# Transposes between groups of experts: one run of three or four tiles on TensorE in place of runs of two, with the third and fourth tile in banks of the first layers' ring

## The chip, the cores and the metric

One NeuronCore of one Trainium2 chip runs the whole program in one launch. The metric is the device time of one execution in microseconds, as the median of several; lower is better. TensorE is called PE here, VectorE DVE, ScalarE ACT, GpSimd POOL and SyncE SP, as in the profile.

## The reference

The program computes sliding-window attention with sink tokens, and feeds its output into a mixture of experts in two levels. Cut to the second part, which the change is in:

```python
x = attention(q, k, v).transpose(0, 2, 1, 3).reshape(3072, 512)
g_idx = argmax(x @ w_group)                   # one of 4 groups, weight g_w = its softmax
e_idx = argmax(xg @ w_expert[g])              # one of 4 experts in it, weight e_w = its softmax
h  = maximum(x[tok] @ w1[g, e], 0.0)          # 512 -> 1024, for the tokens of one expert
ye = h @ w2[g, e]                             # 1024 -> 512
out[tok] = (g_w * e_w)[:, None] * ye
```

All tensors are fp32. There are 16 experts; each token goes through exactly one.

## The kernel before, in words

**Stages.** Attention over 24 tiles of 128 tokens fills the first 150 us or so. Each tile's rows are written to a DRAM scratch, and routing on DVE builds lists of tokens. The experts are then worked off in order of how many tokens they got: r0 is the largest, r15 the smallest, and `CAPT` (L48) gives the slots of each. `PARTS` (L76 to L82) is the list of groups in that order: r0, r1, r8, r2 (in two parts), r9, r3 with r14, r10, r4 with r15, r5, r11, r6 with r12, r7 with r13. The change touches the places between the groups from r9 on.

**Precision.** A weight or an activation is split into a high part (`whi`, rounded to fp32r) and the rest (`wlo`); products hi·hi, hi·lo and lo·hi are summed in PSUM. The split of a 128x1024 block of weights is one cast on ACT (`whi<-rw`) and one subtraction on DVE (`wlo<-rw,whi`); activations are split likewise into a tile `un`. Small experts (r14, r15, at most 64 slots: "plain") and the remainder rows of r3, r4, r8 to r11 (`FEW`) use the raw fp32 weights instead.

**One group.** First layers write to `ph`, a ring of four PSUM banks (L1312). Then come the second layers, tile by tile of 128 tokens, into `po`, a ring of two (L1375): `layer2` (L1133) issues for each of 8 blocks f three matmuls of 512 columns. Where a group's first expert has remainder rows, `layer2` stops after f = 1, and `rest_of` (L1199) and `few_tokens` (L1113) do those rows in 16 matmuls in a bank that `spare()` (L207) takes from the `ph` ring; in the trace they are the `ph<-rw,hq` matmuls. A second ring of two banks, `ps_t` (L1374), holds transposes, and `bank(ps_t)` (L194) takes one.

**The pieces between.** Two kinds of work need PE transposes between the first layer of one group and the first layer of the next. A move, `xpose` (L928), takes 128 gathered token rows of the next group (`xg`, fetched by indirect DMA one group earlier), transposes them in four blocks into one PSUM bank, and has ACT and DVE split them into `un` (for a plain expert ACT copies them to `xr`), and DVE copy the gate `cg`. Rows of a small tile can share the transposes of another (`TWIN`, L90). `hidden_t` (L1084) transposes one half, four blocks, of the hidden layer `hs` of a plain or narrow expert of the present group; ACT (and DVE, if not plain) take them out. `hs` itself is made at the end of that expert's first layer (`layer1_plain`, L1034): ACT copies one strip of PSUM and DVE adds the other strips, one for 64 slots and three for 32 slots, for each half of 512 columns.

**Their order.** The list `todo` of such pieces is cut into runs of two (L1414). A run is issued whole by `pop_todo` (L1099), after every so many blocks f of the second layers, or by `pop_front` (L1105), ahead of the remainder rows at f = 1. Where there are remainder rows, the moves come first in the list, and otherwise the hidden pieces. All engines work in program order (`Pinned`, L126), so a piece that PE must wait for holds up everything behind it on PE. When the weight casts are issued is set by a planner's clock (`spend`, L916), to which each move adds some DVE time.

The pieces at each place, with the rows of each transpose:

- behind r9: r3 (128, 128) and r14 with a twin (96); then runs of 2 and 1
- behind r3 with r14: r10 (128, 32), hidden of r14 (two halves, 64 rows); runs of 2 and 2
- behind r10: r4 (128, 128), r15 with a twin (64); runs of 2 and 1
- behind r4 with r15: r5 (128, 96), hidden of r15 (two halves, 32 rows); runs of 2 and 2
- behind r11: r6 (128, 64), r12 (128); runs of 2 and 1
- behind r6 with r12: hidden of r12 (two halves, 128 rows), r13 (128), r7 (128, 64); runs of 2, 2 and 1

All other places have two pieces or fewer, or are behind r0.

Of the kernel before, what the change touches and what calls it, by code (L numbers as in the profile page):

```python
# [89 lines left out]
TWIN = {(3, 2): (14, 0, 64), (4, 2): (15, 0, 32), (9, 1): (2, 3, 96)}  # L90
# [53 lines left out]
def drain(g):  # L144
    for _ in g:
        pass


def moe_attention(tc, kqT, vN, vS, nsw, wgx, wgd, w1, w2, out):
    nc = Pinned(tc)  # L150
    v = nc.vector
    with ExitStack() as top, ExitStack() as att:
# [9 lines left out]
        ps_t = None  # L162
# [31 lines left out]
        def bank(pt):  # L194
            return pt.tile([P, 4, P], F32, name="tp")
# [11 lines left out]
        def spare():  # L207
            return tail[0].tile([P, 512], F32, name="ph")
# [466 lines left out]
        def dve(us):  # L675
            state["dve"] = max(state["dve"], state["clk"]) + us
# [218 lines left out]
        def routing(k, kinds=(None, "pe", "rd")):  # L895
            while k > 0:
                if not rb or not have.issuperset(rb[0][0]):
                    return False
                kind = rb[0][2] if isinstance(rb[0][2], str) else None
                if kind not in kinds or (kind == "pe" and state["clk"] < state["at"]):  # L900
                    return False
                rb[0][2] = r = next(rb[0][1], "end")
                k -= r if isinstance(r, int) else 1
                if tail:
                    dve(0.6 if kind == "rd" else 0.25)
                state["at"] = max(state["clk"] + state["gap"], state["dve"] + 0.4)
                if rb[0][2] == "end":
                    rb.pop(0)
            return True

        def wait_for(key):
            while key not in ready:
                state["clk"] += 0.3
                routing(1)
# [13 lines left out]
        def xpose(q, j, early=False):  # L928
            r, w = (q["r"], q["j0"] + j), min(P, q["T"] - j * P)
            if r in TWIN:  # L930
                return
            src = xg[r]
            both = [(q, j, 0, w)] + [tenants[a] + b[2:] + (32,) for a, b in TWIN.items() if b[0:2] == r]
            rows = sum(x[3] for x in both)
            tx = spare().rearrange("p (a b) -> p a b", a=NDC) if early else bank(ps_t)
            for c in range(NDC):
                nc.tensor.transpose(tx[:, c, 0:rows], src[0:rows, c * P:(c + 1) * P], ident[0:rows, 0:rows])
            for q, j, p, w in both:
                T, o, t = q["T"], q["o"], tx[:, :, p:p + w]
                dve(0.3 + 0.5 * w / P)  # L940
                cg[q["r"], q["j0"] + j] = gate = gp.tile([P, 1], F32, name="cg", bufs=10)
                if q["plain"]:
                    q["x"] = a = yp.tile([P, NDC, 64], F32, name="xr", bufs=1)[:, :, 0:w]
                    nc.scalar.copy(a, t)
                elif q["r"] in WHOLE:
                    q["x"] = a = yp.tile([P, NDC, q["n"]], F32, name="xw", bufs=1)
                    nc.scalar.copy(a, t[:, :, 0:q["n"]])
                else:
                    a = xx[:, :, o + j * P:o + j * P + w]
                    nc.scalar.copy(a, t)  # L950
                    v.tensor_tensor(xx[:, :, o + T + j * P:o + T + j * P + w], t, a.bitcast(F32), ALU.subtract)
                v.tensor_copy(gate[0:w], src[p:p + w, DM:DM + 1])

        def split_h(q, fs, src):
            T, o, s, m = q["n"], q["o"], q["s"], q["m"]
            e = min(m, T)
            hi = hx[:, fs, o:o + e]
            nc.scalar.activation(hi, src[..., 0:e], AF.Relu)
            dve(0.1 + T / 960)
            yield  # L960
            if m < T:
                v.tensor_scalar(q["hq"][:, fs, 0:T - m], src[..., m:T], 0.0, None, ALU.max)
            for a, z, d in ((0, min(m - s, e), m + s), (m - s, e, s)):
                if z > a:
                    v.scalar_tensor_tensor(hx[:, fs, o + a + d:o + z + d], src[..., a:z], 0.0,
                                           hi[..., a:z].bitcast(F32), ALU.max, ALU.subtract)
# [114 lines left out]
            for c in range(NDC):  # L1081
                held.pop((1, r, c))

        def hidden_t(q, u):  # L1084
            T = q["T"]
            tx = bank(ps_t)
            for c in range(4):
                f = 4 * u + c
                nc.tensor.transpose(tx[:, c, 0:T], q["hs"][0:T, f * P:(f + 1) * P], ident[0:T, 0:T])
            if q["plain"]:  # L1090
                if u == 0:
                    q["h"] = yp.tile([P, NFC, 64], F32, name="hr", bufs=1)[:, :, 0:T]
                nc.scalar.activation(q["h"][:, 4 * u:4 * u + 4], tx[:, :, 0:T], AF.Relu)
                return
            drain(split_h(q, slice(4 * u, 4 * u + 4), tx[:, :, 0:T]))
# [113 lines left out]
        def finish(g):  # L1209
            for us in g:  # L1210
                spend(us)
# [13 lines left out]
        def first_layers(g):  # L1225
            return sorted(g, key=lambda q: q["r"] not in WHOLE)
# [4 lines left out]
        for i in range(NI):  # L1231
            a, b, c = i - 1, i - 2, i - 3
# [81 lines left out]
        a, b, c = NI - 1, NI - 2, NI - 3  # L1314
# [59 lines left out]
        ps_t = fl.enter_context(tc.tile_pool(name="ps_t", bufs=2, space=PSUM, side="left", reuse_waits="tile"))  # L1374
# [7 lines left out]
        for i, g in enumerate(PARTS):  # L1382
            nxt = PARTS[i + 1] if i + 1 < len(PARTS) else []
            if i == 1:
                fetch(nxt)
            todo = []
            for k, q in enumerate(first_layers(g)):
                plan.update(todo=todo, at=0, next=2, every=2)
                if i == 0 and k == 0:
                    finish(ew)  # L1390
                    plan.update(todo=[lambda: xpose(g[1], 0)], at=0, next=6)
                    finish(layer2(q, 0))
                    plan.update(todo=[])
                elif q["T"] > P:
                    finish(layer1_wide(q))
                elif q["plain"]:
                    finish(layer1_plain(q))
                    todo = todo + [lambda q=q, u=u: hidden_t(q, u) for u in range(2)]
                elif q["r"] in WHOLE:
                    finish(layer1_whole(q))  # L1400
                else:
                    finish(layer1_narrow(q))
                    todo = todo + [lambda q=q, u=u: hidden_t(q, u) for u in range(2)]
            for f in todo if g[0]["T"] <= P else []:
                f()
                todo = []
            tot = NFC * (sum((q["m"] + P - 1) // P for q in g if not q["plain"]) - (i == 0))
            if i == 0:
                todo += [lambda: wait_for("x1"), lambda: None]
            moves = [lambda q=q, j=j: xpose(q, j) for q in first_layers(nxt) for j in range(q["nt"]) if (q["r"], q["j0"] + j) not in TWIN]  # L1410
            rem = any(q["m"] < q["T"] for q in g)
            front = (len(moves) + 1) // 2 if rem else 0
            todo = moves + todo if front else todo + moves
            todo = [lambda fs=todo[k:k + 2]: [f() for f in fs] for k in range(0, len(todo), 2)]  # L1414
            if i >= 1 and i + 2 < len(PARTS):
                fetch(PARTS[i + 2])
            front = min(front, 1)
            first = (4 if g[-1]["plain"] else 8) if len(g) > 1 else 2
            plan.update(todo=todo, at=0, next=first, every=(tot - first - 3) / max(1, len(todo) - front), front=front)
            if i == 0:  # L1420
                plan.update(todo=todo[:1], next=2)
            if i + 1 == len(PARTS):
                nc.gpsimd.drain()
                fv = nc.nc.values_load(novi[0:1, 1:2], min_val=0, max_val=MAXO)
            work = [(q, j) for q in g for j in range((q["m"] + P - 1) // P)]
            if i == 0:
                work.pop(0)
            if g[-1]["plain"]:
                work.insert(1, work.pop())
            for q, j in work:  # L1430
                finish(layer2_plain(q) if q["plain"] else layer2(q, j))
                if (j + 1) * P < q["m"]:
                    continue
                if i == 0 and q["r"] == 0 and not q["last"]:
                    plan.update(todo=todo[1:], next=tot - 8, every=1.5)
            for f in plan["todo"]:
                f()
# [241 lines left out]
```

## Time and profile before

| | |
|---|---|
| median of 3 runs | 484.18 us (484.17 to 486.46) |
| the profiled execution | 485.83 us, of which the span (first to last instruction) is 484.1 us |
| PE busy | 465.2 us (96%), 5491 matmuls |
| DVE busy | 370.7 us (77%) |
| ACT busy | 328.1 us (68%) |
| DMA | 117.09 MB, mean 242 GB/s |
| granted PE clock | full in every slice of the page |

The page of the profile gives busy time for each engine and a chain that ended last. Since nearly all instructions are issued through one helper (L119), groups are told apart by tiles and not by lines. The timeline of PE lists matmuls in order of time, and merges neighbours of one kind: a row has its start, how long it lasted to the end of the last matmul in it, and their number. Matmuls are pipelined, so that one lasts longer than the step from one to the next; what a piece costs is read from starts, from the matmul ahead of it to the one behind.

### The profile page before, as it was taken

To read this page: it belongs to the slowest core of one execution; us is meant where nothing else is said; L and a number is where in the kernel's file an instruction comes from. 1 tells how busy PE (TensorE), PEld (TensorE's weight loads), DVE (VectorE), ACT (ScalarE), POOL (GpSimd) and SP (SyncE) were. 2 spreads that over 40 slices of the span, in tenths; PEclk is the share of its full clock that TensorE was granted. 3 is DMA by queue.
4 is the path that set the end of the run, shared out by engine and by line. 5 is a ranking of instruction groups with operands and counts; after the bars stand their busy time and mean duration, and the time that the engine had idled before them with its cause. 6 is when DMAs were issued, how large, how long until landed. Compare 5 with 4: busy or idle time off the path is not lost.

```text
span 484.1 us, 14838 instructions
## 1 busy us (share of the span) xinstructions
PE 465.2 (96%) x5491; PEld 388.5 (80%) x5491; DVE 370.7 (77%) x1182; ACT 328.1 (68%) x866; POOL 179.9 (37%) x274
## 2 busy tenths in 40 slices
PE   8999999998989999999999999999999999999994
PEld 6788878886769888887989789568776977887974
DVE  7676998997989899997714875577687997897380
ACT  6999978998893445686615755367455787776371
POOL 3775775765763142352203124032301813102102
PEclk9999999999999999999999999999999999999999
DMA  7898888889768937835952348497749993995611
GB/s 209 260 273 290 263 252 246 270 278 334 238 220 272 333 108 267 268 126 168 389 210 84 110 174 300 177 332 283 278 176 375 403 340 86 362 374 220 239 39 51
DMA packets 58978, 117.09 MB, mean 242 GB/s; under 512 B 8700, under 2 KB 21116, under 8 KB 58896
## 3 DMA queue, kind: packets, MB, share of 16 engines
q1 hardware_dynamic: 54304, 102.65, 62.5%
q0 software_dynamic: 4320, 13.26, 8.1%
q8 instruction: 45, 0.74, 0.6%
q14 instruction: 37, 0.30, 0.2%
q10 hardware_dynamic: 272, 0.15, 0.1%
HBM read 103.25 MB, written 12.96 MB: 240 GB/s over the span
## 4 chain that ended last, share of the span: by engine, by line
PE 71%; DVE 11%; ACT 7%; issue 5%; POOL 3%; DMA 1%; POOLq 0%; DVEq 0%; ACTq 0%
PE po L119 31%; PE ph L119 30%; PE tp L119 6%; ACT pt L119 4%; PE ps L119 3%; DVE sm L119 2%; DVE wlo L119 2%; POOL pu L119 2%; PE lg L119 2%; ACT whi L119 1%; DMA rw<-in_w 1%; DVE xt L119 1%; ACT pa L119 1%; DVE lt L119 1%; DVE ps L119 1%
## 5 line engine op out<-in xcount | busy, mean ns | idle before, releaser
L119 DVE TENSOR_TENSOR wlo<-rw,whi 128x1024 fp32r<-128x1024 f32 x108 | 130.2, 1223 | 23.9 <-ACT whi L119 19.9
L119 POOL DMA_INDIRECT out<-ot,sidx x32 | 48.6, 1519 | 216.4 <-ACT ot L119 123.8
L119 PE MATMUL ph<-un,whi 128*128 128x256 f32 (+9 forms) x544 | 127.9, 321 | 0.6 <-DVE hc L119 0.5
L119 PE MATMUL po<-whi,un 128*128 128x512 f32 (+5 forms) x384 | 128.1, 397 | 0.0
L119 ACT CAST whi<-rw 128x1024 fp32r<-128x1024 f32 (+1 forms) x111 | 111.7, 1023 | 9.8 <-DMA rw<-in_w 5.3
L119 PE MATMUL ph<-un,wlo 128*128 128x256 f32 (+10 forms) x416 | 98.1, 264 | 0.0
L119 PEld LDWEIGHTS ph<-un,whi 128*128 128x128 f32 x544 | 89.6, 189 | 3.1 <-DVE hc L119 0.7
L119 PEld LDWEIGHTS po<-whi,un 128*128 128x128 f32 (+4 forms) x384 | 70.1, 183 | 25.4 <-issue 6.7
L119 ACT ACTIVATE pt<-sm,st 128x136 f32<-128x136 f32 x192 | 76.0, 402 | 6.0 <-DVE st L119 5.1
L119 PE MATMUL po<-wlo,un 128*128 128x512 f32 (+6 forms) x200 | 77.7, 390 | 0.0
L119 PEld LDWEIGHTS ph<-un,wlo 128*128 128x128 f32 x416 | 76.6, 189 | 1.1
L119 DVE CUSTOM_DVE_ANT_0 sm<-ps,msk 128x136 f32<-128x136 f32 x192 | 45.7, 295 | 7.4 <-ACT spT L119 1.1
L119 DVE TENSOR_TENSOR hc<-ph,hc 128x160 f32<-128x160 f32 (+7 forms) x72 | 24.5, 344 | 24.7 <-ACT hc L119 21.9
L119 PEld LDWEIGHTS po<-wlo,un 128*128 128x128 f32 (+5 forms) x200 | 35.9, 179 | 8.2 <-DVE wlo L119 0.2
L119 PE MATMUL ps<-kb,qb 64*64 64x208 f32 (+1 forms) x768 | 38.8, 334 | 3.2 <-issue 2.5
L119 POOL DMA_INDIRECT xg<-xd,gidx x30 | 34.0, 1134 | 17.2 <-issue 7.2
L119 ACT COPY hc<-ph 128x160 f32<-128x160 f32 (+7 forms) x72 | 22.3, 309 | 22.3 <-PE ph L119 17.5
L119 ACT ACTIVATION_READ_ACCUMULATOR pt<-sm,st 128x1 f32 x192 | 36.8, 192 | 0.0
L119 POOL COPY pu<-spT 32x512 f32<-32x512 f32 x46 | 28.1, 638 | 22.3 <-ACT spT L119 22.1
L119 ACT ACTIVATE ot<-po,cg 128x512 f32<-128x512 f32 (+6 forms) x25 | 17.0, 679 | 26.1 <-PE po L119 26.0
L119 PEld LDWEIGHTS ps<-kb,qb 64*64 64x64 f32 x768 | 26.7, 133 | 8.8 <-issue 3.5
L119 POOL TENSOR_SCALAR_AFFINE_SELECT pu<-pa 64x512 f32<-64x512 f32 x40 | 26.1, 653 | 18.8 <-ACT pa L119 18.8
(199 smaller groups left out, 715.0 us busy)
## 6 DMA issues: line engine op xcount, KB each, us to landing
rw<-in_w SPq DMA_DIRECT2D x128, 512.0 KB
vv<-in_vN SPq DMA_DIRECT2D x24, 512.0 KB
kb<-in_kqT SPq DMA_DIRECT2D x23, 288.0 KB
qb<-in_kqT SPq DMA_DIRECT2D x24, 256.0 KB
xd<-xt SPq DMA_DIRECT2D x24, 256.0 KB
vv<-in_vS SPq DMA_DIRECT2D x24, 128.0 KB
out<-ot,sidx POOLq DMA_INDIRECT x32
xg<-xd,gidx POOLq DMA_INDIRECT x30
```

Source lines behind the costliest of these rows:

```text
L119: r = f(*a, **k)
```

## The change

Three edits. The list `todo` is cut otherwise: behind r1 and later, a list of up to four pieces forms one run, a list of five forms runs of two and three, and behind r0 it stays in twos. Within a run, the third and later pieces are called with `early=True`, and take their bank from the first layers' ring (`spare()`) in place of `ps_t`; `hidden_t` gets that parameter, which `xpose` had already. The lambdas take the flag as an argument.

```diff
-        def hidden_t(q, u):
+        def hidden_t(q, u, early=False):
             T = q["T"]
-            tx = bank(ps_t)
+            tx = spare().rearrange("p (a b) -> p a b", a=4) if early else bank(ps_t)
...
-                    todo = todo + [lambda q=q, u=u: hidden_t(q, u) for u in range(2)]
+                    todo = todo + [lambda e=False, q=q, u=u: hidden_t(q, u, e) for u in range(2)]
...
-                todo += [lambda: wait_for("x1"), lambda: None]
-            moves = [lambda q=q, j=j: xpose(q, j) for q in first_layers(nxt) for j in range(q["nt"]) if (q["r"], q["j0"] + j) not in TWIN]
+                todo += [lambda e=False: wait_for("x1"), lambda e=False: None]
+            moves = [lambda e=False, q=q, j=j: xpose(q, j, e) for q in first_layers(nxt) for j in range(q["nt"]) if (q["r"], q["j0"] + j) not in TWIN]
             rem = any(q["m"] < q["T"] for q in g)
             front = (len(moves) + 1) // 2 if rem else 0
             todo = moves + todo if front else todo + moves
-            todo = [lambda fs=todo[k:k + 2]: [f() for f in fs] for k in range(0, len(todo), 2)]
+            cut = [0, len(todo)] if i and len(todo) <= 4 else [0, 2, len(todo)] if i and len(todo) == 5 else [*range(0, len(todo), 2), len(todo)]
+            todo = [lambda fs=todo[k:z]: [f(n > 1) for n, f in enumerate(fs)] for k, z in zip(cut, cut[1:])]
```

At the first five places of the list above all pieces are now issued at f = 1, ahead of the remainder rows; at the sixth the second run holds r13 and both tiles of r7, and comes at block 15 of 24 in place of 13 and 17.

## Rows read from the trace of the kernel before

**Rows 1.** Chain of waits from 160 us on, shares of that stretch by engine and tile.

```profile
by line: PE ph L119 43.0%; PE po L119 38.4%; PE tp L119 4.3%; issue 2.9%; DVE wlo L119 2.3%; DMA rw<-in_w 2.1%; ACT whi L119 1.7%; POOL out L119 0.8%; DVE un L119 0.6%; ACT un L119 0.6%; DVE hc L119 0.6%; ACT hc L119 0.2%; ACT ot L119 0.2%;
```

**Rows 2.** Waits of PE's matmuls from 160 us on: total us, times, longest.

```profile
PE ph L119 <- DVE hc L119: 0.5, 1, 0.5
PE tp L119 <- DVE cg L119: 0.5, 1, 0.5
```

**Rows 3.** Timeline of PE behind r9: start us, us, what, how many.

```profile
289.73 0.39 PE L119 MATMUL po<-whi,un 128*128 128x512 f32 x1
289.96 0.49 PE L119 MATMUL tp<-ident,xg 96*128 96x96 f32 x4
...
290.55 0.40 PE L119 MATMUL po<-wlo,un 128*128 128x512 f32 x1
```

**Rows 4.** Timeline of PE behind r3 with r14, the run of hidden pieces.

```profile
316.09 0.39 PE L119 MATMUL po<-whi,un 128*128 128x512 f32 x1
316.42 0.71 PE L119 MATMUL tp<-ident,hs 64*128 64x64 f32 x8
...
317.39 0.40 PE L119 MATMUL po<-wlo,un 128*128 128x512 f32 x1
```

**Rows 5.** Timeline of PE behind r10, the run of one tile of 64 rows.

```profile
342.25 0.40 PE L119 MATMUL po<-whi,un 128*128 128x512 f32 x1
342.58 0.46 PE L119 MATMUL tp<-ident,xg 64*128 64x64 f32 x4
...
343.30 0.39 PE L119 MATMUL po<-wlo,un 128*128 128x512 f32 x1
```

**Rows 6.** Timeline of PE behind r4 with r15: moves, remainder rows, hidden run.

```profile
361.26 0.93 PE L119 MATMUL tp<-ident,xg 128*128 128x128 f32 x8
362.12 1.91 PE L119 MATMUL ph<-rw,hq 128*16 128x512 f32 x16
...
366.64 0.40 PE L119 MATMUL po<-whi,un 128*128 128x512 f32 x1
366.96 0.68 PE L119 MATMUL tp<-ident,hs 32*128 32x32 f32 x8
...
367.91 0.40 PE L119 MATMUL po<-wlo,un 128*128 128x512 f32 x1
```

**Rows 7.** Timeline of DVE, sums of the hidden layers of r14 and r15.

```profile
309.94 0.68 DVE L119 TENSOR_TENSOR hs<-hs,ph 64x512 f32<-64x512 f32 x1 [0.18 <-ACT hs L119]
...
359.72 4.26 DVE L119 TENSOR_TENSOR hs<-hs,ph 32x512 f32<-32x512 f32 x6 [0.79 <-ACT hs L119]
```

**Rows 8.** Timeline of PE behind r11; in brackets idle time and its releaser.

```profile
407.54 0.99 PE L119 MATMUL tp<-ident,xg 128*128 128x128 f32 x8
408.46 2.28 PE L119 MATMUL ph<-rw,hq 128*8 128x512 f32 x16
...
411.93 0.39 PE L119 MATMUL po<-whi,un 128*128 128x512 f32 x1
412.78 0.66 PE L119 MATMUL tp<-ident,xg 128*128 128x128 f32 x4 [0.45 <-DVE cg L119]
...
413.51 0.39 PE L119 MATMUL po<-wlo,un 128*128 128x512 f32 x1
```

**Rows 9.** Timeline of DVE behind r11 and in the first layer of r6.

```profile
412.04 0.68 DVE L119 TENSOR_TENSOR un<-tp,un 128x512 fp32r<-128x512 f32 x1
...
417.83 0.36 DVE L119 TENSOR_TENSOR hc<-ph,hc 128x192 f32<-128x192 f32 x1 [0.53 <-ACT hc L119]
418.78 1.22 DVE L119 TENSOR_TENSOR wlo<-rw,whi 128x1024 fp32r<-128x1024 f32 x1 [0.59 <-ACT whi L119]
```

**Rows 10.** PE's longest pause, its clock behind it (windows), and the first matmuls.

```profile
115.53 1.27 PE L119 MATMUL ps<-kb,qb 64*64 64x208 f32 x19 [2.13 <-issue]
...
115.60:121.00 5.40, 5.40 (x126) 4.73 (x127) 4.11 (x21) 3.86 (x16) 3.18 (x5) 1.00 0.96 309
...
1.13 3.38 PE L119 MATMUL tp<-wz 128*128 128x192 bf16 x20 [1.13 <-POOL wz L119]
```

More of the change, by code (lines that the diff above doesn't have):

```diff
@@ L1402, in moe_attention @@
                     finish(layer1_narrow(q))
-                    todo = todo + [lambda q=q, u=u: hidden_t(q, u) for u in range(2)]
+                    todo = todo + [lambda e=False, q=q, u=u: hidden_t(q, u, e) for u in range(2)]
             for f in todo if g[0]["T"] <= P else []:
```

## The prediction

> **What bounds the kernel now.** I read the page's busy shares, then the chain of waits from 160 us on, where the experts begin. TensorE's matmuls `ph`, `po` and `tp` make up 86% of that chain [rows 1]. Then the list of what PE waits for in the same stretch: two waits of half a microsecond are all that concerns the places changed [rows 2]. So here a change is worth what it takes off PE's own stream, or adds to it. Then the timeline of PE at each of the six places, for what a run of transposes costs, and the timelines of DVE there, for when the data of a piece is ready and whether DVE could become the bound.
>
> The unit is one step of the second layers: from a 512-column matmul to what comes behind it are 0.23 us [rows 3]. A run costs the time from the last matmul ahead of it to the second behind it, less two steps (0.46).
>
> **The change place by place.** No transposes are added or dropped: each place gives up one run as such and hangs its transposes behind another. What goes is the way into a run and out of it.
>
> *Behind r9.* The lone 96-row piece costs 290.55 - 289.73 - 0.46 = 0.36 [rows 3]. Appended, it is like the second half of the run behind r4 with r15, which has four 128-row and four 96-row transposes in 362.12 - 361.26 = 0.86 [rows 6]: half of that is 0.43 with the way out, about 0.1 of which the remainder rows need anyway; I take 0.33. Gain 0.03, bounds -0.07 to 0.05.
>
> *Behind r3 with r14.* The hidden run costs 317.39 - 316.09 - 0.46 = 0.84 [rows 4]. Appended, at most the 0.64 from its first transpose to the next matmul, and about 0.5 if the way out is shared with the remainder rows: 0.57. Gain 0.27, bounds 0.20 to 0.34. It now waits for `hs`, which DVE has done at 309.94 + 0.68 = 310.62 [rows 7], about when the moves begin, and the moves take 0.9; so no wait.
>
> *Behind r10.* The lone 64-row piece costs 343.30 - 342.25 - 0.46 = 0.59 [rows 5]. Appended: about half of the 0.92 that four 128-row and four 64-row transposes take behind r11 [rows 8], less some of the way out: 0.40. Gain 0.19, bounds 0.10 to 0.25.
>
> *Behind r4 with r15.* The hidden run costs 367.91 - 366.64 - 0.46 = 0.81 [rows 6]; appended, about the 0.61 from its start to the next matmul: gain 0.20. But it is pulled from 366.96 to behind the moves, which end at 362.12, and its data is not there. r15 has 32 slots, so DVE adds three strips for each half: six additions from 359.72 for 4.26 us, that is until 363.98, the first half by some 361.85 [rows 7]. The first hidden half can go at 362.12; the second must wait until 363.98, and everything behind it on PE with it: the remainder rows (16 matmuls), then r4's second layer. Their start moves from 362.12 to 363.98 plus four short transposes and the way out (0.3 to 0.4), 364.36. Delay 2.24, less the 0.81 that need not be paid later: a loss of 1.43. If the first half's wait covers the whole tile `hs`, four more transposes come late: 1.68. I take 1.45. Nothing hides it, since PE is in order, and nothing behind it could start early. The DMAs that the remainder rows release on SP's queue (they free raw weight buffers) go out 2.2 us later, PE needs them 1.4 us later, so their slack shrinks by 0.8; I count nothing for that, and keep it in the upper bound.
>
> *Behind r11.* The lone 128-row piece costs 413.51 - 411.93 - 0.46 = 1.12 [rows 8]. It waits for one of the two `ps_t` banks, which DVE empties only from 412.04 to 412.72, being late with weight splits [rows 8, 9]. The new bank comes from the first layers' ring, whose tenants have long been read, so the wait goes. Appended, the piece costs half of 0.92 plus the change of width, 0.53: gain 0.59. The remainder rows take 2.28 here against 1.91 elsewhere [rows 6, 8], since the last of their input is late on DVE; starting 0.53 later, they no longer meet that: gain 0.37. Together 0.95. What is late next is DVE, which is busy nearly without a pause from here into r6's first layer; its only pauses there are 0.53 and 0.59, and both wait for ACT work that itself waits for PE [rows 9]. They shrink as PE comes earlier, so DVE can follow by up to 1.1. I keep 0.95, bounds 0 and 0.95.
>
> *Behind r6 with r12.* The last 64-row piece loses its own run (0.59 as behind r10, [rows 5]) and is appended ahead of full-width matmuls, where the way out is paid in full: 0.5 to 0.6. Gain 0.05, bounds 0 to 0.19.
>
> *Queues and the planner.* ACT and DVE get the evacuations of a run in a burst; they are the same instructions, and the third ones come ahead of the remainder rows' output and not behind it. The moves' share of the planner's DVE time is added at f = 1 at once. Casts near these places come at the same blocks, so I expect their order to stay, but for a block or so behind r6. The remainder rows and the next first layer shift by one or two banks in the ring of four; those banks are emptied well before. POOL's gathers come one group ahead and are not touched. All this at nothing; if a cast slips into another place in a first layer, PE may gain or lose one wait such as the 0.5 [rows 2], either way.
>
> Sum: -0.03 - 0.27 - 0.19 + 1.45 - 0.95 - 0.05 = -0.04 us. The durations come from the execution of 485.83 us (span 484.1), which lies 1.65 above the median of 484.18; I apply the difference to the median: 484.1 us, no change.
>
> **The rivals.** (1) *The gain behind r11 is given back*: DVE bounds from 408 us to the end of r6's first layer, and PE, come early, waits there for the sums `hc`. Place: r6's first layer; price 0.95; it decides if the two pauses of DVE [rows 9] stay as they are. For it: DVE has little else to give, and PE's other wait in rows 2 is of this kind, for `hc`. Against it: both pauses end on ACT work that moves with PE. Time 484.18 + 0.91 = 485.1, slower than before by 0.2%.
>
> (2) *The wait for r15's hidden layer does not come*, because the sums are done earlier or the order on PE lets other work ahead: only the gains remain, 0.03 + 0.27 + 0.19 + 0.20 + 0.95 + 0.05 = 1.7, 482.5 us. Against it: the additions are one chain on DVE with no gap, and the program order is fixed.
>
> (3) *PE's clock falls at the long run.* Behind r4 with r15, PE would do moves, a pause of about 1.6 us and more transposes, some 3.1 us without one matmul that multiplies. If the clock dropped to its lower level and needed as long to rise as the first matmuls at the start took (20 in 3.38 us, 0.17 us for 192 columns, which is the lower level of 1.2 GHz [rows 10]), half of 3.4 us would be lost: 484.1 + 1.7 = 485.8 us. Against it: the longest pause, 2.13 us, left the granted clock at 1.00 in the stretch behind it [rows 10]; but that pause has matmuls at both sides and no run of transposes, so it does not settle it.
>
> (4) *Ways in and out cost nothing*: what sets the price is the change of width between transposes and matmuls, and that stays when a run moves, so the gains of 0.03, 0.27, 0.19, 0.20 and 0.05 fail, and behind r11 only the wait (some 0.6) and the remainder rows' 0.37 are won. Then 1.65 - 0.6 - 0.37 = +0.7, where 1.65 is the loss behind r4 with r15 without its 0.20: 484.9 us. For it: the way into a 128-row or 96-row run is one plain step, 289.96 - 289.73 = 0.23 [rows 3]. Against it: into a 64-row run it is 342.58 - 342.25 = 0.33 [rows 5], and the second step behind each run is longer than 0.23 too. The Trainium skill speaks for this rival in "TensorE: Matmul & The Clock Gate", section "Part 2: What happens when you issue a matmul": PE's queue may pull a weight load ahead of matmuls that still run, so that the next stationary operand is in place when its turn comes. By that rule the first transpose of a run follows without a gap, which rows 3 show and rows 5 do not, and by it alone the time would be this rival's 484.9.
>
> **How the numbers follow.** Forecast 484.1 (its own range 483.5 to 484.8): 0.55. Rival 1: 0.17. Rival 2: 0.10. Rival 3: 0.06. Rival 4: 0.07. The remaining 0.05 is for a shift of the planner's order worth more than 2 us. The range runs from 482.4, rival 2 with it, to 486.0, which takes in rivals 1, 3 and 4 and the upper bounds. About 0.5% (2.4 us) is what a measurement tells from no change; all cases but the last lie inside it, though rivals 2 and 3 come near its ends. So faster by more than that 0.04, within it 0.91, slower 0.05.
>
> **What would show it.** In the changed trace: PE behind r4 with r15 idle for some 1.6 us between the two hidden halves, released by DVE `hs`, and the remainder rows 2.2 us later behind the moves; behind r11 no wait for DVE `cg` in front of the third tile, and remainder rows of about 1.9 us; behind r3 with r14 sixteen transposes in one run with no pause. From r10's first layer PE should be some 0.3 us earlier than before, in r5's first layer about 1.0 later, and in r6's first layer even. The prediction is wrong if the hidden halves of r15 don't wait, if PE's waits for DVE `hc` in r6's first layer grow, or if the granted clock leaves 1.00 behind 362 us.

## The result, and the profile after

The change makes the kernel slower by half a per cent: median 488.47 us against 485.73 of the kernel before (22 runs of each), ratio 1.0052 with an interval of 1.0033 to 1.0071, which is 1.6 to 3.4 us. The ratio leaves out the runs that lie more than 1.5% above the fastest of their kernel, three of the 22 with the change. The forecast was 484.1, with a range that ended at 486.0.

| | before | after |
|---|---|---|
| profiled execution, us | 485.83 | 488.23 |
| its span, us | 484.1 | 486.5 |
| PE busy, us | 465.2 | 467.1 |
| mean granted PE clock | 0.999 | 0.994 |

A table of starts on PE tells where the time went. It has the first matmul of each stretch, read from the timelines of PE in both traces, so that only the change of the last column from line to line counts:

| starts, us | before | after | after later by |
|---|---|---|---|
| second layer of r9 | 284.23 | 285.33 | 1.09 |
| first layer of r3 | 293.12 | 294.18 | 1.06 |
| second layer of r3 | 309.18 | 310.24 | 1.05 |
| second layer of r14 | 318.65 | 319.51 | 0.86 |
| second layer of r10 | 336.76 | 337.44 | 0.68 |
| first layer of r4 | 345.86 | 346.36 | 0.50 |
| first layer of r15 | 357.90 | 359.38 | 1.47 |
| second layer of r15 | 369.17 | 372.15 | 2.98 |
| second layer of r11 | 406.15 | 409.13 | 2.98 |
| first layer of r6 | 416.08 | 418.16 | 2.08 |
| end of the last changed place | 448.63 | 450.65 | 2.02 |

The 1.09 on top is not of the change: up to there both programs issue the same. In attention the granted clock of the changed kernel's execution was down once, as its windows show (us from:to, length, busy us of PE, PEld, DVE, ACT and POOL with counts, clock, DMA share, GB/s). The second row is the stretch behind r4 with r15, at full clock:

```profile
142.86:146.28 3.42, 3.42 (x56) 2.88 (x56) 2.44 (x8) 2.20 (x7) 2.59 (x4) 0.50 0.51 169
...
366.00:370.20 4.20, 4.20 (x27) 2.26 (x26) 2.24 (x7) 1.63 (x3) 0.00 (x0) 1.00 0.99 373
```

The six changed places themselves: r9 -0.03, r3 with r14 -0.20, r10 -0.18, r4 with r15 +1.51, r11 -0.90, r6 with r12 -0.06, together +0.14. From the second layer of r14 to that of r10, where nothing was changed, 0.18 are gained. And there is a line that no step of the forecast has: the first layer of r4, where nothing was changed either, takes 0.97 longer. PE's waits in the experts show both losses (total us, times, longest; these answer to [rows 2]):

```profile
PE ph L119 <- DVE hs L119: 1.5, 1, 1.5
PE ph L119 <- PE ph L119: 0.8, 1, 0.8
PE ph L119 <- DVE oh L119: 0.7, 1, 0.7
PE ph L119 <- DVE hc L119: 0.3, 1, 0.3
```

The first is the pause that was forecast; the wait for `cg` of [rows 2] is gone; the second is new and comes at the end of r4's first layer; the third is in both kernels. Now the timeline of PE from there on (start, us, what, count, in brackets idle time and its releaser), which answers to [rows 6]:

```profile
359.38 1.92 PE L119 MATMUL ph<-rw,xr 128*32 128x512 f32 x16 [0.79 <-PE ph L119]
...
362.73 0.93 PE L119 MATMUL tp<-ident,xg 128*128 128x128 f32 x8
363.59 0.43 PE L119 MATMUL ph<-ident,hs 32*128 32x32 f32 x4
365.57 0.40 PE L119 MATMUL ph<-ident,hs 32*128 32x32 f32 x4 [1.55 <-DVE hs L119]
365.90 1.91 PE L119 MATMUL ph<-rw,hq 128*16 128x512 f32 x16
...
370.89 0.40 PE L119 MATMUL po<-wlo,un 128*128 128x512 f32 x1
```

From the moves to the matmul that stood behind the old hidden run are 370.89 - 362.73 = 8.16 us, against 367.91 - 361.26 = 6.65 in [rows 6]: 1.51 lost. DVE's six additions end at 361.17 + 4.26 = 365.43, in the row that answers to [rows 7], and the second half follows at 365.57:

```profile
361.17 4.26 DVE L119 TENSOR_TENSOR hs<-hs,ph 32x512 f32<-32x512 f32 x6 [0.66 <-ACT hs L119]
```

Behind r3 with r14, sixteen transposes without a pause, for the run of [rows 4], and behind r10 the 64-row tile that stood alone in [rows 5]; behind r11 twelve transposes with no wait for `cg`, and the remainder rows at their plain 1.90, for [rows 8]. All on PE:

```profile
311.74 0.96 PE L119 MATMUL tp<-ident,xg 128*128 128x128 f32 x8
312.63 0.71 PE L119 MATMUL ph<-ident,hs 64*128 64x64 f32 x8
313.27 1.92 PE L119 MATMUL ph<-rw,hq 128*24 128x512 f32 x16
...
338.84 1.04 PE L119 MATMUL tp<-ident,xg 128*128 128x128 f32 x8
339.81 0.46 PE L119 MATMUL ph<-ident,xg 64*128 64x64 f32 x4
340.20 1.92 PE L119 MATMUL ph<-rw,hq 128*24 128x512 f32 x16
...
410.52 0.99 PE L119 MATMUL tp<-ident,xg 128*128 128x128 f32 x8
411.44 0.66 PE L119 MATMUL ph<-ident,xg 128*128 128x128 f32 x4
412.03 1.90 PE L119 MATMUL ph<-rw,hq 128*8 128x512 f32 x16
```

DVE in r6's first layer has pauses of 0.31 and 0.59 (0.53 and 0.59 in [rows 9]): 

```profile
419.92 0.36 DVE L119 TENSOR_TENSOR hc<-ph,hc 128x192 f32<-128x192 f32 x1 [0.31 <-ACT hc L119]
420.86 1.22 DVE L119 TENSOR_TENSOR wlo<-rw,whi 128x1024 fp32r<-128x1024 f32 x1 [0.59 <-ACT whi L119]
```

Last, ACT in r4's first layer. In the kernel before its four casts of w2 start at 349.33, 350.82, 352.32 and 353.81, with no wait for a DMA. Now the last two wait, and with them everything queued behind them on ACT:

```profile
353.97 1.05 ACT L119 CAST whi<-rw 128x1024 fp32r<-128x1024 f32 x1 [1.05 <-DMA rw<-in_w]
354.93 0.38 ACT L119 ACTIVATE un<-ph 128x256 fp32r<-128x256 f32 x1
356.55 1.05 ACT L119 CAST whi<-rw 128x1024 fp32r<-128x1024 f32 x1 [1.25 <-DMA rw<-in_w]
357.51 0.65 ACT L119 ACTIVATE un<-ph 128x256 fp32r<-128x256 f32 x2
```

The evacuations `un<-ph` stand in ACT's queue behind a cast whose weights have not landed; the `ph` banks stay full, and PE waits. That is a load that comes too late, and the loads of this layer are released by the remainder rows behind r10, which the third tile now precedes: these rows start 345.86 - 339.13 = 6.73 us ahead of r4's first layer before, and 346.36 - 340.20 = 6.16 after. The eight loads follow on SP's queue (first before, then after):

```profile
340.22 4.87 SPq L119 DMA_DIRECT2D rw<-in_w  x8
...
341.29 4.96 SPq L119 DMA_DIRECT2D rw<-in_w  x8
```

The first goes out 5.64 us ahead of r4's first layer before, and 5.07 after.

So the trace leaves three questions. Does the pause behind r4 with r15 alone make the 0.5%? Does r10's third tile make r4's first layer late? And is one execution of the kernel before a fair base, when both traces have waits of which some may be chance?

### The profile page after: what moved, and what is told of

Same layout as the page of the kernel before. It is cut to its first block, busy times and chain, and to the rows that moved or that the text cites. A ratio compares the mean times of both kernels' runs of the same rounds, so it can differ in the third digit from the quotient of the medians.

```text
span 486.5 us, 14844 instructions
## 1 busy us (share of the span) xinstructions
PE 467.1 (96%) x5491; PEld 390.9 (80%) x5491; DVE 371.0 (76%) x1182; ACT 328.5 (68%) x866; POOL 181.2 (37%) x274
## 4 chain that ended last, share of the span: by engine, by line
PE 70%; DVE 13%; ACT 7%; issue 4%; POOL 3%; DMA 1%; POOLq 0%; SPq 0%; DVEq 0%; ACTq 0%
PE ph L119 31%; PE po L119 31%; PE tp L119 5%; ACT pt L119 3%; DVE sm L119 3%; PE ps L119 3%; ACT whi L119 2%; DVE wlo L119 2%; POOL pu L119 1%; DVE xt L119 1%; PE lg L119 1%; DMA rw<-in_w 1%; DVE lt L119 1%; DVE ps L119 1%; ACT pa L119 1%
## 5 line engine op out<-in xcount | busy, mean ns | idle before, releaser
L119 POOL DMA_INDIRECT out<-ot,sidx x32 | 49.8, 1556 | 216.2 <-ACT ot L119 127.9
L119 PE MATMUL po<-whi,un 128*128 128x512 f32 (+5 forms) x384 | 126.4, 395 | 0.0
```

What stands on the lines that cost most here:

```text
L119: r = f(*a, **k)
```

## The experiments

The places of each profile are read as in the table, against the profiled execution of the kernel before unless another is named.

**e0_null: the kernel before, unedited.**

> The kernel before once more, unchanged, against itself: how much two sets of runs of one program differ. Both theories: no difference, 0.0 us, within 0.3%. PE's milestones behind 150 us should stand at the same distances from one another as in the trace of before (within 0.1 us from the first layer of r1 to the last layer), while the attention part ahead of them may shift by 1 us or so.

486.43 against 486.24 us, ratio 1.0009 [0.9982, 1.0036]. Its trace is the more useful half. PE behind r11, and PE's waits in the experts:

```profile
406.97 1.90 PE L119 MATMUL ph<-rw,hq 128*8 128x512 f32 x16
...
410.74 0.66 PE L119 MATMUL tp<-ident,xg 128*128 128x128 f32 x4 [0.27 <-DVE cg L119]
```

```profile
PE ph L119 <- DVE un L119: 0.9, 1, 0.9
PE ph L119 <- DVE oh L119: 0.7, 1, 0.7
PE tp L119 <- DVE cg L119: 0.3, 1, 0.3
```

The remainder rows take 1.90 here, not the 2.28 of [rows 8], and the bank wait is 0.27, not 0.45; r10's first layer is 0.73 shorter. So two executions of one kernel differ by more than the 0.1 expected at these places. The 0.37 and 0.18 are missing in f1, f2, f3 and f4 too, where r11 is as before, but g1 has them again: its place is only 0.03 shorter than in the execution on which the forecast rests. Five of seven traces lack them, so against a usual execution r11's gain is 0.90 - 0.55 = 0.35, and against the mean of the seven about 0.5.

**e1_after: the change itself once more.**

> The changed kernel once more. Theory P (the places): the trace's steps from one place to the next hold again: r9 -0.04, r3 -0.20, r10's first layer and moves -0.35, r4's first layer +0.97, r15's hidden run +1.51, r11 -0.90, r6 and r12 -0.06, sum +0.9 us; the rest of the measured 2.5 us is from the attention part, which is the same program, and so not from the change: a ratio of about 1.002. Theory A (the attention part is hit too): the change makes PE's clock fall in the attention tail at 143 us in nearly every run, some 1 to 1.5 us more: a ratio of about 1.005 again, with the clock's fall in this trace and not in that of e0_null.

489.59 against 486.24 us, ratio 1.0065 [1.0031, 1.0099]. r9 -0.04, r3 with r14 -0.20, r10 -0.17, r4's first layer +0.87, r11 -0.90, r6 with r12 -0.06: all as in the first trace but one, r4 with r15 at +3.08. PE there, and its windows:

```profile
363.34 0.43 PE L119 MATMUL ph<-ident,hs 32*128 32x32 f32 x4
365.32 0.40 PE L119 MATMUL ph<-ident,hs 32*128 32x32 f32 x4 [1.55 <-DVE hs L119]
365.66 2.56 PE L119 MATMUL ph<-rw,hq 128*16 128x512 f32 x16
368.15 0.80 PE L119 MATMUL po<-whi,un 128*128 128x512 f32 x1
```

```profile
355.00:366.78 11.78, 9.44 (x77) 6.55 (x79) 9.69 (x22) 4.62 (x11) 0.00 (x0) 1.00 0.47 162
366.78:370.20 3.42, 3.42 (x13) 1.68 (x6) 1.16 (x2) 0.93 (x2) 0.00 (x0) 0.50 0.99 376
370.20:376.00 5.80, 5.80 (x34) 3.37 (x33) 2.98 (x4) 2.88 (x4) 2.63 (x2) 1.00 0.84 255
```

The pause is the same 1.55. But 1.5 us behind it the granted clock falls to 0.50, the level of 1.2 GHz, for 3.42 us in which PE has work without a break: 3.08 - 1.51 = 1.6 us more. This is rival 3. In the first trace it did not happen. Neither theory of the expectation holds: the clock stays at 1.00 through attention here, and the time is further above before than the places of the first trace give.

**e2_no_r15 and e3_no_r10_r15: the change without r4 with r15, and without r10 as well.**

```diff
-cut = [0, len(todo)] if i and len(todo) <= 4 else ...
+cut = [0, len(todo)] if i and i != 8 and len(todo) <= 4 else ...            # e2
+cut = [0, len(todo)] if i and i not in (7, 8) and len(todo) <= 4 else ...   # e3
```

> The change everywhere but behind r4 with r15, where the runs stay in twos. Theory P: the 1.51 us there go, all else stays: sum -0.6 us against before, ratio 0.9988, PE's pause between the two hidden halves of r15 gone, and r4's first layer still 0.97 late. Theory A: 1 to 1.5 us above that, ratio about 1.001.

> The change everywhere but behind r10 and behind r4 with r15. Theory P with the loads as the cause of the late first layer of r4 (the remainder rows of r10 come 0.39 us later with a third tile ahead of them, the weight loads that they release come later, and a cast that waits for its load holds up ACT): that loss of 0.97 goes with the third tile, and so does the gain of 0.18 there: sum -1.4 us, ratio 0.997. If the late first layer comes from elsewhere (the ring, or the DMAs by chance), it stays late by about 1 us: sum -0.4 us. Theory A: 1 to 1.5 us above either.

e2: 486.74 against 486.24, 0.9987 [0.9953, 1.0020]; no pause, no fall of the clock behind 362 us, r4's first layer +1.40. e3: 485.99, 0.9993 [0.9962, 1.0023]; r4's first layer +0.00, r11 -0.90. So the slowdown as a whole needs the place r4 with r15, and in these two traces r4's first layer is as before again when r10 is. Neither kernel is measurably faster than before.

**f1_only_r10: only r10's place changed** (`if i == 7` in both conditions).

> The change behind r10 alone. If the third tile ahead of the remainder rows is what makes r4's first layer late: PE gains some 0.2 us behind r10, and from the start of r4's first layer to r15's first layer it loses 0.9 to 1.4, with an ACT cast there that waits over 1 us for its load; sum about +0.9 us, ratio 1.002. If the late first layer needs the other places too, nothing but the gain: -0.2 us.

486.03 against 485.49, 1.0008 [0.9984, 1.0033]. The place gains 0.18 and r4's first layer loses 1.17, with two casts on ACT that wait for their loads:

```profile
352.61 1.05 ACT L119 CAST whi<-rw 128x1024 fp32r<-128x1024 f32 x1 [0.89 <-DMA rw<-in_w]
...
355.54 1.05 ACT L119 CAST whi<-rw 128x1024 fp32r<-128x1024 f32 x1 [1.60 <-DMA rw<-in_w]
```

**f2_r10_dummy: the kernel before with four matmuls on zeros, which add nothing to the result, ahead of r10's remainder rows.**

```diff
 def pop_front():
+    if plan["dummy"]:                 # i == 7
+        warm(4, spare()[:, 0:192])
```

> The kernel before, with four dummy matmuls on zeros (192 columns, about 0.1 us each) between the moves behind r10 and the remainder rows; the tile of r15 stays where it was. If the remainder rows' delay and with it the late weight loads are the cause: PE is 0.4 us later from there, and r4's first layer loses a further 0.9 to 1.4 us, with the cast of w2's last block waiting for its load. If the cause is the order of the third tile's work on ACT and DVE: r4's first layer takes as long as before, and the sum is +0.4 us.

485.99 against 485.49, 0.9997 [0.9965, 1.0028]. PE loses 0.33 there, but r4's first layer only 0.15: the expectation fails, and by its design. The dummies come on top, so the remainder rows and r4's first layer are late together, and the remainder rows stay 6.74 ahead; the third tile, taken from behind them, cuts that to 6.16. The run doesn't tell the theories apart.

**f3_only_r15: only r4 with r15** (`if i == 8`).

> The change behind r4 with r15 alone. Both theories: PE's pause between the two hidden halves, 1.5 us lost in that place, r4's first layer as before. If PE's clock falls behind the pause in a part of the executions, this kernel's time is 1.5 to 3 us above before (ratio 1.003 to 1.006) and its profile may show the half clock from some 367 us on, for 1.6 us more; if that one fall was by chance, 1.5 us, ratio 1.003.

488.69 against 485.49, 1.0064 [1.0028, 1.0100]: this one place is enough for the whole slowdown. Its place reads +3.13, again with the clock at 0.50 behind the 1.55 us pause:

```profile
367.61:371.03 3.42, 3.42 (x15) 1.16 (x8) 0.45 (x3) 0.79 (x2) 0.00 (x0) 0.50 1.02 362
```

This speaks against r10's third tile as the only cause: r4's first layer is +1.09 here, with r10 unchanged and the first load 5.65 ahead as before, and ACT's fourth cast waits 2.26 for its load. It can be late by itself.

**f4_r15_late: only r4 with r15 (`if i == 8`), in one run, but behind the remainder rows, at block 5.**

```diff
-front = min(front, 1)
+front = 0 if i == 8 else min(front, 1)
```

> Behind r4 with r15 alone all four pieces in one run, but at block 5 of r4's second layers, behind the remainder rows, when r15's hidden sums are done. If the pause comes from the data and not from the length of the run: sixteen transposes in a row without a pause, PE gains 0.2 to 0.3 us there against before, no fall of the clock, ratio 0.9995. If a long run of transposes is what costs (by the clock or else), PE loses there in this kernel too.

485.93 against 485.49, 0.9983 [0.9952, 1.0013]. The same sixteen transposes in one run, without a pause, and in this profile the granted clock stays at 1.00 behind them:

```profile
368.27 0.93 PE L119 MATMUL tp<-ident,xg 128*128 128x128 f32 x8
369.13 0.68 PE L119 MATMUL ph<-ident,hs 32*128 32x32 f32 x8
...
370.20:376.00 5.80, 5.80 (x34) 3.37 (x33) 3.97 (x8) 4.79 (x7) 1.28 (x1) 1.00 1.02 375
```

The place costs 0.00 and not the -0.2 expected: the remainder rows now have a way in and out of their own. r4's first layer is +0.69, r10 unchanged.

**g1_r15_fill: only r4 with r15 (`if i == 8`), its two hidden halves kept apart by fourteen matmuls on zeros, which add nothing to the result.**

```diff
 def hidden_t(q, u, early=False):
+    if early and u:
+        warm(14, spare()[:, 0:192])
```

> Behind r4 with r15 alone the one run as in the change, with 14 dummy matmuls on zeros between the two hidden halves, where PE otherwise pauses for 1.5 us. They do no work that the output needs. If the clock falls because of the pause: PE loses the same 1.5 us or slightly more in that place, but the granted clock stays at full behind it in the profile, and the time is nearer to before than that of the kernel without them (ratio about 1.003 against 1.006). If the clock falls for another reason, the half clock shows some 2 us behind the run here too.

487.50 against 486.53, 1.0019 [0.9990, 1.0048]. PE, and the window behind:

```profile
364.19 0.43 PE L119 MATMUL ph<-ident,hs 32*128 32x32 f32 x4
364.55 1.33 PE L119 MATMUL ph<-wz 128*128 128x192 bf16 x14
366.17 0.40 PE L119 MATMUL ph<-ident,hs 32*128 32x32 f32 x4 [0.29 <-DVE hs L119]
366.51 1.91 PE L119 MATMUL ph<-rw,hq 128*16 128x512 f32 x16
```

```profile
366.00:370.20 4.20, 4.03 (x28) 2.23 (x29) 2.24 (x7) 1.03 (x3) 0.00 (x0) 1.00 1.04 380
```

The place still loses 1.50, since the second half waits for the same sums, but with work in the pause the clock holds in this trace. That points to the idle pause and away from the transposes alone. It is one profile, though, and the first trace of the change kept 1.00 with the pause left idle, so it is not shown.

**g2_swap_r3_r4: the change, with the remainder rows ahead of the run behind r3 and r4, and r10 in twos as before.**

```diff
-pop_front()
+if not plan["swap"]: pop_front()
 yield from rest
+if plan["swap"]: pop_front()          # plan["swap"] = i in (6, 8)
...
-cut = [0, len(todo)] if i and len(todo) <= 4 else ...
+cut = [0, len(todo)] if i and i != 7 and len(todo) <= 4 else ...
```

> The change, but behind r3 with r14 and behind r4 with r15 the remainder rows go ahead of the run of four, and behind r10 the runs stay in twos. Places theory: r15's hidden sums end when the moves behind the remainder rows do, so no pause over 0.2 us and no fall of the clock; r9 -0.04, r3 about -0.3, r4 with r15 about -0.2, r11 -0.35 to -0.9, r6 with r12 -0.06: sum -1.0 to -1.5 us, ratio 0.997 to 0.998. If a run of sixteen transposes itself costs, the place behind r4 with r15 loses over 0.5 us still.

485.88 against 486.53, 0.9971 [0.9934, 1.0008]. r9 -0.03, r3 with r14 -0.05, r4 with r15 -0.03, r11 -0.90, r6 with r12 -0.06, r4's first layer +0.27; no pause for `hs`, no fall of the clock in the experts. For r3 with r14 and r4 with r15 some -0.3 and -0.2 were expected; that these do not come fits f4, where the remainder rows had a way in and out of their own.

**g3_swap_all: the change with the remainder rows ahead of the run behind r9, r3, r10 and r4** (`plan["swap"] = i in (5, 6, 7, 8)`, all pieces in one run).

> As the kernel before this one, but behind r9 and r10 too all pieces in one run behind the remainder rows. Places theory: the remainder rows of r10 come 1 us sooner, the weight loads that they release too, and r4's first layer is not late for its load (12.0 us long, the cast of w2's last block on time). Against that the remainder rows of r9 and r10 meet hidden columns that DVE has not written yet and wait some 0.5 to 0.8 us each. Sum about 0, between -1 and +0.6 us.

485.96 against 486.53, 0.9984 [0.9955, 1.0013]. r9 and r10 lose 0.62 and 0.63, since their remainder rows now come before DVE has made `hq`: in this trace of PE they take 2.59 and not 1.92.

```profile
284.85 2.59 PE L119 MATMUL ph<-rw,hq 128*32 128x512 f32 x16
287.37 1.09 PE L119 MATMUL tp<-ident,xg 128*128 128x128 f32 x8
288.30 0.50 PE L119 MATMUL ph<-ident,xg 96*128 96x96 f32 x4
```

But r10's remainder rows start 8.24 ahead of r4's first layer, with all three tiles behind them, and that layer takes 12.04 as before. The theory of the loads expects this; but the layer takes 12.04 in most traces with r10 unchanged too, so this one trace adds little.

**h1_swap_r3_r4_again: the kernel of g2 once more, on its own.**

> The version with the remainder rows ahead of the run behind r3 and behind r4, once more, against new runs of before. If the places hold: again r9 -0.04, r3 -0.04, r4 with r15 -0.03, r6 with r12 -0.05, and behind r11 -0.35 against the usual execution of before (-0.9 against the profiled one); no pause for DVE hs and no half clock behind r4 with r15. The sum is -0.5 us against the usual execution of before (about -1.4 against the profiled one), so a ratio of 0.997 to 0.999. If the 0.9971 of the first set was chance, 1.000 or above.

484.08 against 486.87, 0.9956 [0.9925, 0.9987]: the only set here whose interval stays below one, and the best; that of g2, the same kernel, reached 1.0008. PE's waits in the experts are down to one:

```profile
PE ph L119 <- DVE oh L119: 0.7, 1, 0.7
```

```profile
365.38 1.91 PE L119 MATMUL ph<-rw,hq 128*16 128x512 f32 x16
367.22 0.99 PE L119 MATMUL tp<-ident,xg 128*128 128x128 f32 x8
```

Behind r4 the remainder rows fill PE while DVE adds up `hs`. How much faster it is stays loose: its places give some -0.5 us against a usual execution of before, the two sets say -1.4 (g2) and -2.1 (h1), and the second interval does not reach -0.5.

## Why the prediction was wrong

**The ledger.** Against a usual execution of before, the places give -0.03 (r9) - 0.20 (r3 with r14) - 0.18 (r10) + 0.9 (r4's first layer, below) + 1.5 (the pause) - 0.35 (r11) - 0.06 (r6 with r12) = +1.6 us. The fall of the clock comes on top, at 1.6 where it happens. In two of three profiles it did, which would make +1.1 and a sum of +2.7; by the mean clocks below it is nearer one execution in five, +0.3 and a sum of +1.9. Measured are 0.0052 x 485.73 = 2.5, between 1.6 and 3.4, so the times do not tell which. The parts agree with the same sums: e3 -0.6 (measured -0.3), f1 +0.7 (+0.4), f3 +1.8 to +2.6 (+3.1), g1 +1.5 (+0.9), each inside its interval, which is 1.2 to 1.75 us wide to either side. From the forecast's -0.04 to the lower sum it is 0.9 for loads counted at nothing, 0.6 at r11, 0.3 for the clock and 0.1 for the rest: three steps failed, and the pause was none of them.

**The size of the pause was right; what follows it was not.** The forecast took 1.45 for r4 with r15; 1.51 was measured, with the pause between the halves, released by DVE `hs`, as described. What failed here is the judgement on rival 3, at a chance of 0.06 and against a row: the 2.13 us pause with a clock of 1.00 behind it [rows 10]. That row is one execution. In the same stage six of the fourteen profiles have the clock at 0.50 for 3.42 us, and PE's longest pause in the 10 us ahead of these falls was 0.9 to 1.8 us, shorter than that 2.13.

Here the pause lies in a run of transposes, and in two of three profiles the clock went to 0.50 for 3.42 us, 1.5 us behind the pause in e1 and 1.0 in f3; price 1.6, as rival 3 had worked out (1.7). g1, with matmuls in the pause, and f4, with the transposes but no pause, kept 1.00, in one profile each; the first trace, with pause and transposes, kept it too. So it is not shown that it takes the two together. The Trainium skill had a sentence for it: "TensorE: Matmul & The Clock Gate", section "Part 4: PE-mode transpose", says that transposes do not count as busy time for the clock in the way matmuls do. e1 and f3 agree with it; no run here puts an equal stretch of multiplying matmuls ahead of an idle pause at this place, so it is not shown apart. Why the first trace escaped is not shown either: its instructions and its pause are the same.

How often the fall comes can be estimated from the mean granted clock, which is on record for each execution. It is 0.9946 on average over all 46 executions with the idle pause (after, e1, f3) and 0.9953 over the 116 of before that ran beside the experiments. One fall takes 3.42 x 0.5 / 486 = 0.0035 off such a mean. The difference, 0.0007 with 0.0009 to either side, makes a fall in about one execution of five, and in fewer than one of two; falls elsewhere in the program are in both means. By this estimate two of three profiles were a high draw, and the fall is the smallest of the three steps.

**"At nothing" for the DMAs failed, at a place where it was not even asked.** The forecast named the loads that the remainder rows release behind r4 with r15, and counted nothing; there it held: one cast on ACT waits 0.94 for its load, at 369.53, and no matmul of PE waits from there to 400 us. Behind r10, where the third tile was moved ahead of the remainder rows, it counted only the 0.40 of PE's time. With the tile ahead, r4's first layer takes 13.01, 12.92, 13.44 and 13.21 us (after, e1, e2, f1); with it elsewhere 12.04, 12.04, 12.04, 12.19, 12.73, 13.13, 12.21, 12.31 and 12.04 (before, e0, e3, f2, f4, f3, g1, g2, h1), and 12.04 in g3, where the remainder rows come first. The means of the two groups are 13.15 and 12.28 (g3 with the second), hence the 0.9 of the ledger.

The traces bear out the way from tile to load. The first load goes out 5.07 or 5.08 us ahead of r4's first layer in all four traces with the tile, and 5.64 or 5.65 in the others but g3 (7.15). The third of ACT's four casts waits for its load in all four (0.38 to 1.05), and of the ten others in g2 alone (0.35). But the fourth cast waits in the four and in seven of the ten. The third tile makes late what is sometimes late anyway; in f3 and f4 the first loads went out as before, and what delays the fourth stays open. The medians are too loose to show the 0.9: f1 is +0.4, and e2, with the tile, is 0.3 below e3.

**r11: the mechanism was right, the base was not.** 0.95 was forecast, 0.90 came in both traces of the change: no bank wait, remainder rows at 1.90. But 0.55 of it were waits of the one execution read, which e0 and f1 to f4 lack and g1 has again; the match of 0.90 with 0.95 is partly luck of that base. A saving that consists of removed waits needs a second trace of the same kernel before it is counted.

**What held.** r9 (0.03 forecast, 0.03 measured), r3 with r14 (0.27, 0.20: its lower bound), r10's own run (0.19, 0.18), r6 with r12 (0.05, 0.06). Rival 1 did not come: PE does not wait for `hc` in r6's first layer, where one of DVE's pauses shrank as forecast. Rival 2 did not come. Rival 4 fails at r3 with r14 and at r10, where the ways did cost what the rows gave; by the rule of the Trainium skill that the forecast cited ("TensorE: Matmul & The Clock Gate", section "Part 2: What happens when you issue a matmul": weight loads pulled ahead), read as rival 4 read it, these gains would have been nil. The measurement differs from that reading for these runs, and decides.

**The level.** The median of three runs, 484.18, lay below every larger set of the kernel before (485.49 to 486.87). The forecast shifted its sum down to it; that is 1.5 us of the 4.4 by which the number missed, and no part of the effect. Taken from 484.18, the measured 2.5 would give 486.7, still above the range.

## What to carry to other kernels

Before a group of instructions is moved up an in-order queue, look up when the producer of its last operand ends: a pause of 1.5 us was easy to see and to size, and putting the ready work (the remainder rows) in front removed it. Count a pause of TensorE inside transposes at its length plus what a fall of the clock behind it would cost, times how often that may come, and do not rule the fall out by one execution without it. And for every instruction that a move delays, follow what its end releases: here 0.56 us on the remainder rows came back as 0.9 us on average, by way of a DMA, a cast and the evacuations queued behind the cast.

## What the runs showed of the hardware that was not expected

- Behind a pause of 1.55 us next to transposes the granted clock was at 0.50 for 3.42 us in two of three profiles, though the profiled execution of the kernel before kept 1.00 behind one of 2.13 us [rows 10]. In both the fall comes behind the pause, while PE is busy again.
- The clock fell to 0.50 between 120 and 152 us too, in six of the fourteen profiles (after, e2, f3, f4, g1, h1), where all kernels issue the same program. A lower mean clock of one execution (0.994 against 0.999) is no sign of the change; the place where it fell is.
- Two executions of the same kernel (the profiled one and e0) differed by 0.73, 0.37 and 0.18 us in three places of PE's stream.
